# A gated mix of attention and a GLU: SBUF addresses at multiples of 512 bytes, and the splitting of row maxima moved from VectorE to GpSimd with the transpose one period later

## The chip, the cores and the metric

The kernel runs on one core of one Trainium2 chip. The metric is the device time of one execution in microseconds (us). The kernel before took 1719.04 us, the median of 3 runs (1718.17 to 1721.21).

The engines are named as in the profile: PE is TensorE's matmul, PEld its weight load, DVE is VectorE, ACT ScalarE, POOL GpSimd, and SP the queue engine that issues the DMAs.

## What is computed

```python
x = A_x                                              # 2048 tokens, D = 512
g = _sigmoid((x * gate_w).sum(-1, keepdims=True))
a = _A_ref(x, A_wqkv, A_wo)       # softmax attention, 32 heads of 16
b = _B_ref(x, B_w_gate, B_w_up, B_w_down)   # (sigmoid(x Wg) * (x Wu)) Wd, F = 1792
return g * a + (1 - g) * b
```

In the attention, `scores = q k^T * 16 ** -0.5` are taken through a softmax over all 2048 keys, and the result multiplies `v`. All of it is in fp32.

## The kernel before, in words

[...]

The softmax needs the largest score of each row before the exponential. Attention thus makes the scores twice. The first pass (`sm_step`, L271) multiplies queries by keys (PE L284) for 128 queries and 512 keys at a time and takes the maximum of each row (DVE L286). Sixteen such maxima per row block fill one *part*: pair of heads p, chunk c of 512 queries, half b of the pair. There are 16 pairs, 4 chunks and 2 halves, 128 parts. When a part is full, `turn_max` (L294) makes it usable:

- DVE L298 reduces the four key ranges to one maximum for each row, tile `mx`, 128x4;
- DVE L300 casts it to its high half, in the tile `msq`; DVE L301 subtracts to get the low half (both inputs in SBUF);
- DVE L305 transposes 128x128 of `msq` into a tile `mt`, in blocks of 32;
- `send` issues four small DMAs on SP (L311) that put the two halves, as two rows, under the queries in the tile `QS`.

The second pass (`st_part`, L561) multiplies keys by queries (PE L570); with the two extra rows, the matmul itself subtracts the row's maximum. ACT L572 takes the exponential into tiles `p`. `values` (L692) multiplies `p` by v (32 matmuls at PE L702), ACT L707 copies the result out of PSUM, and POOL L720 adds it to a running sum that a DMA later stores.

All of this runs in a main loop of 256 *periods* (k in `range(NPER)`, L774). A period handles 512 queries of two heads against 512 keys: `emit` follows an order written out by hand, in one string for even and one for odd k:

```python
    STEADY = ("m1 t0 t0 d1 d1 m0 t0 d1 d1 m0 m0 d1 d1 t0 work d1 t0 t0 d1 t0 d1 d1 m0 d1 t0 d1 m0 m0 m1",
              "m0 t1 t1 d0 m1 d0 t1 d0 d0 m1 t1 d0 d0 m1 work d0 t1 d0 m1 t1 d0 t1 d0 t1 d0 d0 m1 m1 m0")
```

Here `m0` and `m1` are one step of the first pass for half 0 or 1, `t0` and `t1` one step of the second, `d0` and `d1` two dense matmuls (PE L150 or L170, on half the array each) of the projections and of the GLU, and `work` takes one job from a list, `later`, of small jobs for GpSimd and SP (splits of weights, mixing of operands, sums of products, stores). Each period has eight of the maxima (DVE L286) and eight exponentials. The matmuls of the passes share seven PSUM banks, handed out by a table, `REUSE`.

What ends a period, in this order: `turn_max` for the part that is full (one is, at the end of each odd period), three or four jobs of `later`, then `values(k)`. The `send` of a part is put at the head of `later`, and comes out of it near the end of the next period.

SP takes its DMAs in program order and waits where one has to: for the data that it stores, or for a buffer that it fills.

Ahead of the loop lie dummy matmuls (PE L84), the first projections (PE L137) and the first maxima; there, `turn_max` and its `send` follow at once. The last eight periods have no maxima and no dense work. Behind the loop come the output projections and the GLU's down-projection (PE L137 and L901).

The tiles are placed in SBUF one behind the other in the order of their making. `warm` is 4 bytes wide per partition, and four others that come early (`logit`, `g1`, `g0`, `mx`) are small too, so that the large tiles behind them start at addresses that are 32 over a multiple of 64 bytes. Ahead of all lies a scratch for dynamic transfers, of the default size of 16384 bytes.

Of the kernel before, what the change touches and what calls it, by code (L numbers as in the profile page):

```python
# [12 lines left out]
F32 = mybir.dt.float32  # L13
F32R = mybir.dt.float32r
AF = mybir.ActivationFunctionType
ALU = mybir.AluOpType
# [8 lines left out]
S, D, H, DH, F = 2048, 512, 32, 16, 1792  # L25
P = 128
KT = D // P
NS = S // P
# [21 lines left out]
def gated_mix(ctx, tc, x, xc, xmix, wqk, wv, wo, w_gu, w_down, gate_w, out):  # L50
    nc = tc.nc
    pe, act, dve, pool, sp = nc.tensor, nc.scalar, nc.vector, nc.gpsimd, nc.sync

    ctx.enter_context(tc.manual_schedule(engines=ORDERED))
    keep = ctx.enter_context(tc.tile_pool(name="keep", bufs=1))
# [3 lines left out]
    def turns(tiles):  # L59
        turn = iter(range(1 << 30))  # L60
        return lambda: tiles[next(turn) % len(tiles)]
# [15 lines left out]
    pv_d = dram.tile([NC, NPAIR, P, 256], F32, name="pv_d")  # L77
    rec_d = dram.tile([P, 512], F32, name="rec_d")

    warm = keep.tile([P, 1], F32, name="warm")  # L80
    dve.memset(warm, 0.0)
    z = warm.bitcast(F32R)
    for _ in range(WARM):
        pe.matmul(banks[2], z.to_broadcast([P, P]), z.to_broadcast([P, 512]), start=True, stop=True)  # L84
    den = keep.tile([P, 512], F32, name="den")
    logit = keep.tile([P, NS], F32, name="logit")
    g1 = keep.tile([P, NS], F32, name="g1")
    g0 = keep.tile([P, NS], F32, name="g0")

    def big(name, dt=F32):  # L90
        return keep.tile([P, 2048], dt, name=name, tag="big", bufs=4)

    def mid(name, dt=F32):
        return keep.tile([P, 4, 512], dt, name=name, tag="mid", bufs=3)

    def split(h, l, src, hi, lo):
# [86 lines left out]
    later = []  # L183
# [5 lines left out]
    def work(n):  # L189
        while later and n:  # L190
            later.pop(0)()
            n -= 1
# [3 lines left out]
    QS, KS = zip(*[(big(f"qs{b}", F32R), big(f"ks{b}", F32R)) for b in range(2)])  # L196
# [51 lines left out]
                    yield sp.dma_start((QS, KS)[t][p % 2][r:r + DH, cols].bitcast(F32), src[a, rows, cols])  # L248

    act.activation(g1[:, :1], warm, AF.Exp)  # L250
    square = turns([(keep.tile([P, 4], F32, name=f"mx{i}"), keep.tile([P, 40], F32R, name=f"msq{i}")) for i in range(1)])
    for _ in range(1):
        pool.memset(square()[1].bitcast(F32), 0.0)
    ones = v.rearrange("p t (h c) -> p t h c", c=VW)[:, :, :, DH]
    pool.memset(ones, 1.0)
    q0 = raw_cols(wqk, 0, "q0", act)
# [10 lines left out]
    stat = {}  # L267
# [3 lines left out]
    def sm_step(j):  # L271

        p, s = divmod(j, 32)
        qt, kh = divmod(s, 2)
        qs, ks = QS[p % 2], KS[p % 2]

        def one(b, i):
            part = (p, qt // 4, b)
            if part not in stat:
                stat[part] = keep.tile([P, 4, 4], F32, name=f"stat{p}_{qt // 4}_{b}", tag="stat", bufs=6)  # L280
                count[part] = 0
            r, g = 64 * b, 2 * kh + i
            t = bankm()
            pe.matmul(t, qs[r:r + KM, qt * P:(qt + 1) * P], ks[r:r + KM, g * 512:(g + 1) * 512],  # L284
                      start=True, stop=True)
            dve.tensor_reduce(stat[part][:, qt % 4, g:g + 1], t, axis=AX.X, op=ALU.max)  # L286
            count[part] += 1
            if count[part] == 16:
                full.append(part)
        return one  # L290

    full = []

    def turn_max():  # L294
        part = full.pop(0)
        p, i, b = part
        m, hl = square()
        dve.tensor_reduce(m, stat.pop(part), axis=AX.X, op=ALU.max)  # L298
        two = hl[:, :8].rearrange("p (t c) -> p t c", c=2)
        dve.tensor_copy(two[:, :, 0], m)  # L300
        dve.tensor_tensor(two[:, :, 1], m, two[:, :, 0].bitcast(F32), ALU.subtract)  # L301
        f = hl.bitcast(F32)
        blocks = bass.AP(f.tensor, f.offset, [f.ap[0], (2, 4), (1, 32)])
        mt = keep.tile([P, 4, 32], F32, name=f"mt{p}_{i}_{b}", tag="mt", bufs=2)
        dve.transpose(mt, blocks)  # L305

        def send():
            r = 64 * b + 3 * DH
            rows = QS[p % 2][r:r + 2, i * 512:(i + 1) * 512].bitcast(F32).rearrange("a (t g j) -> a g t j", g=4, j=32)
            for g in range(4):  # L310
                sp.dma_start(rows[:, g], mt[32 * g:32 * g + 2])  # L311
        return send

    SIDES = (slice(0, 64), slice(64, 128))
    def mixing(pair):
# [245 lines left out]
    def st_part(k, b):  # L561

        p, r = divmod(k, 16)
        c, kt = divmod(4 * r, 16)
        qs, ks = QS[p % 2], KS[p % 2]
        r = 64 * b
        pt = ptile[k, b] = mid(f"p{k}_{b}")
        for a in range(4):
            o = bank()
            pe.matmul(o, ks[r:r + KR, (kt + a) * P:(kt + a + 1) * P], qs[r:r + KR, c * 512:(c + 1) * 512],  # L570
                      start=True, stop=True)
            act.activation(pt[:, a, :], o, AF.Exp, scale=DH ** -0.5)  # L572
            yield

    ahead = st_part(0, 1)
    bank = bankm
    for t in range(2, NS, 2):
        two = [Sum(bankv(), tokens(t + a)) for a in range(2)]
        for g in (LOW, UP):
            first_max()  # L580
            for m in range(3 * KT):
                two[0].half(g)
                two[1].half(1 - g)
                if m == 5 or m == 8 and (g == LOW or t == 2):
                    first_max()
                if t == NS - 2 and (g, m) in ((LOW, 8), (UP, 2), (UP, 5), (UP, 8)):
                    next(ahead)
                while full:
                    turn_max()()
            if g == LOW:  # L590
                turn(*two)
            if t >= 12:
                work(1)
        if t < NS - 2:
            for a in range(2):
                put_v(t + a, two[a].o, act)


    seven = [maxb[0], maxb[1], banks[2], maxb[2], banks[1], maxb[3], banks[0]]
    bank7 = turns(seven)  # L600
    chunks = [(c, f) for c in range(NC) for f in range(0, NF, 2)]
# [131 lines left out]
    def dense(g):  # L733
        while True:
            if run:
                run.half(g)
            yield

    count_given = [0]

    def place():
        b = given[-REUSE[count_given[0] % len(REUSE)]]
        count_given[0] += 1
        given.append(b)
        return b

    def emit(order, **parts):

        for word in order.split():
            if word == "turn":  # L750
                if run:
                    turn(run)
            elif word == "work":
                work(1)
            else:
                if next(parts[word], place) is place:
                    place()
# [12 lines left out]
    for a, engine in enumerate((act, dve)):  # L770
        put_v(NS - 2 + a, two[a].o, engine)
    bank = bankm = place
    backlog = []
    for k in range(NPER):  # L774
        n = 2 * k
        if n + FIRST == NSTEP:
            bank = bank7
        if 320 <= n < 448 and n % 16 == 0:
            logit_load((n - 320) // 8)
        if n % 32 == 0 and n // 32 + 1 < NPAIR:  # L780
            pair = load_pair(n // 32 + 1)
        if n % 32 <= 10:
            list(islice(pair, 2))
        if k >= NPER - TAIL:
            group["t0"], group["t1"] = st_part(k, 0), st_part(k + 1, 1) if k + 1 < NPER else iter(())
        elif k % 2 == 0:
            group["t0"] = chain(st_part(k, 0), st_part(k + 1, 0))
        else:
            group["t1"] = chain(st_part(k, 1), st_part(k + 1, 1))
        emit(STEADY[k % 2] if k < NPER - TAIL else LAST[k - NPER], **group)  # L790
        turned = []
        while full:
            turned.append(turn_max())
        if run is None:
            pass
        elif run.done():
            run = next(fill, None)
        else:
            turn(run)
        backlog.append(len(later))  # L800
        work(3 if isinstance(run, Sum) and k % 2 else 4)
        later[:0] = turned
        if 320 <= n < 448:
            t = (n - 320) // 16 * 2
            if n % 16 == 2:
                logit_terms(t, 0)
                logit_terms(t, 1)
            elif n % 16 in (8, 10):
                logit_sum(t, (n % 16 - 8) // 2)
        if EARLY <= k < EARLY + 4:  # L810
            early_exp(*divmod(k - EARLY, 2))
        if k == NPER - 1:
# [78 lines left out]
    for n, (c, f) in enumerate(chunks):  # L891
# [4 lines left out]
        hl = ready[n]  # L896
# [68 lines left out]
```

## Time and profile before

| | |
|---|---|
| median of 3 runs | 1719.04 us (1718.17 to 1721.21) |
| the profiled execution | 1718.9 us |
| its span in the profile | 1717.1 us |
| its mean granted clock | 0.997 |
| PE L702, one period's | 32 matmuls, in 1.92 us |
| DVE L286, the maxima | 2048 of 0.68 us |
| ACT L572, the exponentials | 2048 of 0.63 us |

A row of the timeline reads: start in us from the span's start, length in us, engine, line, operation, out<-in, sizes, how many in a row are merged (x), and in brackets how long the engine stood idle before it and what ended that. A row of a group of instructions reads: line, engine, operation, count | busy us in all, mean ns of one | idle us of the engine just before them. Busy time overlaps itself on PE, because the next matmul begins before the one before it has left the array. The granted clock is the share of its full speed that PE had.

### The profile page before, as it was taken

How to read it: one execution, taken by the hardware profiler on the slowest of the kernel's cores; microseconds unless marked ns; L12 is line 12 of the kernel's file. 1: busy time of each engine (PE TensorE's matmuls, PEld its weight loads, DVE VectorE, ACT ScalarE, POOL GpSimd, SP SyncE). 2: the span in 40 equal slices, each digit the busy share in tenths (PEclk: the TensorE clock that was granted, in tenths of full speed). 3: DMA queues.
4: the chain of work that ended last, by engine and by line, in shares of the span. 5: the costliest groups of instructions: out<-in, count | busy, mean ns of one | idle time of the engine just before them, and what ended most of it. 6: DMA issues, size and time to landing. Idle time of an engine off the chain costs nothing.

```text
span 1717.1 us, 43465 instructions
## 1 busy us (share of the span) xinstructions
PE 1702.4 (99%) x16552; PEld 1129.9 (66%) x16552; DVE 1498.5 (87%) x2706; ACT 1338.0 (78%) x2668; POOL 974.4 (57%) x936
## 2 busy tenths in 40 slices
PE   9999999999999999999999999999999999999999
PEld 7866666666666666666666666666666666578887
DVE  6999999999999999999999999999999999566543
ACT  4188787888888888888888889999888888863321
POOL 1045654347787777766665677677676665252110
PEclk9999999999999999999999999999999999999999
DMA  9524575363544454442347232524242423176752
GB/s 256 113 78 167 164 249 155 114 168 119 137 124 132 134 137 122 128 117 69 100 152 213 85 100 92 120 76 123 64 122 75 104 81 110 42 264 223 238 188 70
DMA packets 125008, 228.54 MB, mean 133 GB/s; under 512 B 19008, under 2 KB 35648, under 8 KB 121792
## 3 DMA queue, kind: packets, MB, share of 16 engines
q1 hardware_dynamic: 124512, 225.24, 45.0%
q8 instruction: 131, 2.15, 0.5%
q14 instruction: 77, 0.63, 0.1%
q10 hardware_dynamic: 288, 0.52, 0.1%
HBM read 149.42 MB, written 75.76 MB: 131 GB/s over the span
## 4 chain that ended last, share of the span: by engine, by line
PE 92%; DVE 6%; DMA 1%; ACT 0%; POOL 0%; issue 0%; SPq 0%; POOLq 0%; ACTq 0%
PE dn L170 26%; PE sm L702 20%; PE sm L284 8%; PE st L284 7%; PE sm L901 7%; PE st L702 6%; PE dn L150 4%; DVE stat L286 4%; PE st L137 4%; PE sm L570 3%; PE st L570 2%; PE dn L901 2%; PE st L150 2%; DVE msq L301 1%; DVE mt L305 0%; PE st L84 0%
## 5 line engine op out<-in xcount | busy, mean ns | idle before, releaser
L286 DVE TENSOR_REDUCE stat<-sm 128x1 f32<-128x512 f32 x1124 | 723.2, 677 | 44.2 <-PE st L570 18.7
L572 ACT ACTIVATE p<-sm 128x512 f32<-128x512 f32 x1217 | 688.4, 631 | 11.3 <-PE sm L570 5.9
L286 DVE TENSOR_REDUCE stat<-st 128x1 f32<-128x512 f32 x924 | 602.2, 676 | 33.6 <-PE sm L570 16.6
L572 ACT ACTIVATE p<-st 128x512 f32<-128x512 f32 x831 | 501.5, 636 | 7.4 <-PE dn L150 3.1
L170 PE MATMUL dn<-xm,mh 64*128 64x512 f32 x1568 | 490.9, 392 | 0.0
L570 PE MATMUL sm<-qs,ks 64*128 64x512 f32 x1217 | 456.2, 411 | 3.8 <-DVE stat L286 3.5
L284 PE MATMUL sm<-ks,qs 48*128 48x512 f32 x1124 | 422.7, 424 | 0.3 <-ACT p L572 0.3
L284 PE MATMUL st<-ks,qs 48*128 48x512 f32 x924 | 369.6, 430 | 0.0
L702 PE MATMUL sm<-p,v 128*17 128x256 f32 x6080 | 366.8, 382 | 0.1
L570 PE MATMUL st<-qs,ks 64*128 64x512 f32 x831 | 331.8, 415 | 5.4 <-DVE stat L286 5.4
L720 POOL TENSOR_TENSOR sum<-sum,part 128x256 f32<-128x256 f32 x192 | 141.3, 736 | 320.0 <-ACT part L707 282.6
L170 PEld LDWEIGHTS dn<-xm,mh 64*128 64x128 f32 x1568 | 290.2, 185 | 42.1
L170 PE MATMUL dn<-xm,ml 64*128 64x512 f32 x784 | 308.8, 394 | 0.0
L702 PEld LDWEIGHTS sm<-p,v 128*17 128x17 f32 x6080 | 160.3, 97 | 166.5 <-ACT p L572 53.7
L284 PEld LDWEIGHTS sm<-ks,qs 48*128 48x128 f32 x1124 | 198.9, 185 | 87.8 <-DVE stat L286 52.7
L570 PEld LDWEIGHTS sm<-qs,ks 64*128 64x128 f32 x1217 | 218.2, 186 | 33.3 <-DVE stat L286 14.6
L284 PEld LDWEIGHTS st<-ks,qs 48*128 48x128 f32 x924 | 165.5, 185 | 84.5 <-DVE stat L286 54.3
L403 POOL TENSOR_TENSOR m<-m,m 128x512 f32<-128x512 f32 x140 | 178.1, 1287 | 4.8 <-ACT m L505 4.8
L570 PEld LDWEIGHTS st<-qs,ks 64*128 64x128 f32 x831 | 152.4, 185 | 26.8 <-DVE stat L286 14.0
L170 PEld LDWEIGHTS dn<-xm,ml 64*128 64x128 f32 x784 | 144.6, 184 | 17.7
L123 POOL TENSOR_TENSOR ml<-r,mh 128x512 fp32r<-128x512 f32 x112 | 143.9, 1285 | 7.7
L505 ACT ACTIVATE m<-dn 128x512 f32<-128x512 f32 x196 | 134.0, 684 | 0.0
(225 smaller groups left out, 2201.0 us busy)
## 6 DMA issues: line engine op xcount, KB each, us to landing
r<-in_w_gu_dram SPq DMA_DIRECT2D x112, 256.0 KB
gul<-gu_d SPq DMA_DIRECT2D x56, 512.0 KB
gu_d<-m SPq DMA_DIRECT2D x84, 256.0 KB
xm_d<-xm SPq DMA_DIRECT2D x32, 512.0 KB
xm<-xm_d SPq DMA_DIRECT2D x32, 512.0 KB
xm<-in_xmix_dram SPq DMA_DIRECT2D x24, 512.0 KB
qs<-q_d SPq DMA_DIRECT2D x90, 128.0 KB
ks<-k_d SPq DMA_DIRECT2D x90, 128.0 KB
```

What stands on the lines that cost most here:

```text
L123: pool.tensor_tensor(l, src, h.bitcast(F32), ALU.subtract)
L150: mm = pe.matmul(self.o, a[rows], b[rows], start=(self.n == 0), stop=(self.n == 2 * len(self.ops) - 1))
L170: pe.matmul(self.o, a, b, start=(self.n == 0), stop=(self.n == len(self.ops) - 1))
L284: pe.matmul(t, qs[r:r + KM, qt * P:(qt + 1) * P], ks[r:r + KM, g * 512:(g + 1) * 512], start=True, stop=True)
L286: dve.tensor_reduce(stat[part][:, qt % 4, g:g + 1], t, axis=AX.X, op=ALU.max)
L403: pool.tensor_tensor(o, x, y, op)
L505: leave = lambda e, o: act.activation(e, o, AF.Copy)
L570: pe.matmul(o, ks[r:r + KR, (kt + a) * P:(kt + a + 1) * P], qs[r:r + KR, c * 512:(c + 1) * 512], start=True, stop=True)
L572: act.activation(pt[:, a, :], o, AF.Exp, scale=DH ** -0.5)
L702: pe.matmul(o[r:r + VW, :], v[:, 4 * k % 16 + a, h * VW:(h + 1) * VW], pts[b][:, a, 256 * i:256 * i + 256], start=(a == 0), stop=(a == 3))
L720: pool.tensor_tensor(s, s, e, ALU.add)
L901: pe.matmul(down[t], a, b, start=(f == 0 and m == 0), stop=(f == NF - 2 and m == 5))
```

## The change

It has three parts.

1. *Addresses and scratch.* `warm` is padded to 96 columns; `logit`, `g1` and `g0` become rows of one tile `gates`; the maxima and their halves lie in one tile `mxs` with two slots of 64 columns (the maximum in columns 40 to 43, the halves in 0 to 7), where `mx` and `msq` were one each. The scratch for dynamic transfers is 2048 bytes. All tiles now start at multiples of 512 bytes. There are 8 buffers for `stat` in place of 6.
2. *Who splits.* `turn_max` falls into `close_max` (the row maximum, on VectorE as before), `halves` (the cast and the subtraction, now on GpSimd, by `split`) and `turned` (the transpose on VectorE), which hands back `send`.
3. *When.* The row maximum stays at the end of odd period k. `halves` goes into a new list, `urgent`, which the next `work` word (in period k + 1) empties ahead of `later`. The transpose stands at the end of period k + 2, ahead of the row maximum of the part that is full there. Its `send` goes into `urgent` too, and comes at the `work` word of period k + 3. Ahead of the loop, one part at a time is closed, halved at once, and transposed and sent four steps later.

With `send` out of `later`, one place more in it is free in every second period, and the jobs behind it come a little earlier in the program.

```diff
-    warm = keep.tile([P, 1], F32, name="warm")
+    warm = keep.tile([P, 96], F32, name="warm")
     dve.memset(warm, 0.0)
+    warm = warm[:, :1]
...
-    logit = keep.tile([P, NS], F32, name="logit")
-    g1 = keep.tile([P, NS], F32, name="g1")
-    g0 = keep.tile([P, NS], F32, name="g0")
+    gates = keep.tile([P, 8, NS], F32, name="gates")
+    logit, g1, g0 = [gates[:, i, :] for i in range(3)]
...
-    square = turns([(keep.tile([P, 4], F32, name=f"mx{i}"), keep.tile([P, 40], F32R, name=f"msq{i}")) for i in range(1)])
-    for _ in range(1):
-        pool.memset(square()[1].bitcast(F32), 0.0)
+    mxs = keep.tile([P, 2, 64], F32R, name="mxs")
+    square = turns([(mxs[:, i, 40:44].bitcast(F32), mxs[:, i, :40]) for i in range(2)])
+    pool.memset(mxs.bitcast(F32), 0.0)
...
-    def turn_max():
+    def close_max():
         part = full.pop(0)
         p, i, b = part
         m, hl = square()
         dve.tensor_reduce(m, stat.pop(part), axis=AX.X, op=ALU.max)
         two = hl[:, :8].rearrange("p (t c) -> p t c", c=2)
-        dve.tensor_copy(two[:, :, 0], m)
-        dve.tensor_tensor(two[:, :, 1], m, two[:, :, 0].bitcast(F32), ALU.subtract)
...
+        def halves():
+            split(two[:, :, 0], two[:, :, 1], m, pool, pool)
+
+        def turned():
+            f = hl.bitcast(F32)
+            blocks = bass.AP(f.tensor, f.offset, [f.ap[0], (2, 4), (1, 32)])
+            mt = keep.tile([P, 4, 32], F32, name=f"mt{p}_{i}_{b}", tag="mt", bufs=2)
+            dve.transpose(mt, blocks)
...
+        return halves, turned
...
             elif word == "work":
+                while urgent:
+                    urgent.pop(0)()
                 work(1)
...
-        turned = []
+        jobs = [turned() for turned in stages.pop(0)]
+        stages.append([])
         while full:
-            turned.append(turn_max())
+            halves, turned = close_max()
+            jobs.append(halves)
+            stages[1].append(turned)
...
-        later[:0] = turned
+        urgent.extend(jobs)
...
-    nc = bacc.Bacc("TRN2", target_bir_lowering=False, num_devices=1)
+    nc = bacc.Bacc("TRN2", target_bir_lowering=False, num_devices=1, dynamic_dma_scratch_size=2048)
```

The lines of the kernel after, for the same things: the row maximum is L298, the halves are L100 and L101 (in `split`), the transpose is L308, the sends L314; the lines behind have moved by 4 (dense loads and sums), by 13 (`values`, L715; the add, L733).

How this stands in the program: first VectorE, at the end of an odd period in which a part of pair 6 is full. The numbers in the names tell the buffers apart; `stat6_0_1` are the sixteen maxima of pair 6, chunk 0, half 1. Before:

```order
L286 TENSOR_REDUCE stat6_0_0_7947<-st0_65 128x1
L298 TENSOR_REDUCE mx0_111<-stat6_0_1_7776 128x4
L300 CAST msq0_112<-mx0_111 128x4
L301 TENSOR_TENSOR msq0_112<-mx0_111,msq0_112 128x4
L305 STREAM_TRANSPOSE mt6_0_1_8064<-msq0_112 128x128
L286 TENSOR_REDUCE stat6_1_1_8095<-st2_67 128x1
```

VectorE after, at the end of a like period of the same pair:

```order
L286 TENSOR_REDUCE stat6_1_0_8255<-st1_66 128x1
L308 STREAM_TRANSPOSE mt6_0_0_8373<-mxs_109 128x128
L298 TENSOR_REDUCE mxs_109<-stat6_1_1_8084 128x4
L286 TENSOR_REDUCE stat6_2_1_8405<-sm1_70 128x1
L286 TENSOR_REDUCE stat6_1_0_8255<-sm0_69 128x1
```

Of the four instructions in a row two are left on VectorE, and the transpose is that of the part before (chunk 0, half 0), ahead of the row maximum of the new one (chunk 1, half 1).

GpSimd after, at a `work` word of an even period, with the two halves between a step of the mixing (L346, L334) and the values' sum (L733):

```order
L346 CAST xm_1_2_6860<-xm_1_2_6860 128x512
L334 TENSOR_TENSOR xm_1_2_6860<-xm_1_2_6860 128x512
L100 CAST mxs<-mxs 128x4
L101 TENSOR_TENSOR mxs<-mxs 128x4
L733 TENSOR_TENSOR sum_3_7044<-sum_3_7044,part_7120 128x256
L407 TENSOR_TENSOR den<-m_0_2_0_7014,m_0_2_0_7096 128x512
```

In GpSimd's order before, neither L100 nor L101 stands at these places.

SP, in pair 1, where the sends of chunk 3, half 0 (`mt_3_0`) stand. Around them are the loads and stores of operands of the dense products (`xm`, `q_d` and `k_d` in HBM). Before:

```order
L722 DMA pv_d<-sum_1_2605 128x256
L311 DMA qs_104<-mt_3_0_2814 2x4x32 x4
L351 DMA xm_1_3614<-xm_d 128x2x512 x2
L331 DMA xm_d<-xm_2_2_2819 256x1x512
L351 DMA xm_1_3614<-xm_d 128x2x512 x2
L321 DMA xm_3_0_3060<-in_xmix_dram 128x512
L238 DMA q_d<-qh_2_2976 128x512
L238 DMA q_d<-qk_1_0_0_2974 128x512
L311 DMA qs_102<-mt_0_1_2972 2x4x32 x4
```

SP after, the same stretch:

```order
L735 DMA pv_d<-sum_1_2597 128x256
L355 DMA xm_0_3126<-xm_d 128x2x512
L355 DMA xm_1_3603<-xm_d 128x2x512 x2
L335 DMA xm_d<-xm_2_2_2737 256x1x512
L355 DMA xm_1_3603<-xm_d 128x2x512 x2
L325 DMA xm_3_0_3051<-in_xmix_dram 128x512
L238 DMA q_d<-qh_2_2965 128x512
L238 DMA q_d<-qk_1_0_0_2963 128x512
L314 DMA qs_102<-mt_3_0_2960 2x4x32 x4
```

The sends of chunk 3, half 0 now stand where those of the next pair's chunk 0, half 1 stood: behind the loads and stores of one more turn.

More of the change, by code (lines that the diff above doesn't have):

```diff
@@ L279, in one @@
             if part not in stat:
-                stat[part] = keep.tile([P, 4, 4], F32, name=f"stat{p}_{qt // 4}_{b}", tag="stat", bufs=6)
+                stat[part] = keep.tile([P, 4, 4], F32, name=f"stat{p}_{qt // 4}_{b}", tag="stat", bufs=8)
                 count[part] = 0
@@ L299, in turn_max, with send @@
         two = hl[:, :8].rearrange("p (t c) -> p t c", c=2)
[L300 to L312, printed above, removed]
+        def halves():
[5 more added lines that the diff above has]
+            dve.transpose(mt, blocks)
+            def send():
+                r = 64 * b + 3 * DH
+                rows = QS[p % 2][r:r + 2, i * 512:(i + 1) * 512].bitcast(F32).rearrange("a (t g j) -> a g t j", g=4, j=32)
+                for g in range(4):
+                    sp.dma_start(rows[:, g], mt[32 * g:32 * g + 2])
+            return send
+        return halves, turned
     SIDES = (slice(0, 64), slice(64, 128))
@@ L573, in st_part @@
             yield
+    closed = []
     ahead = st_part(0, 1)
@@ L587, in gated_mix @@
                     next(ahead)
-                while full:
-                    turn_max()()
+                if closed:
+                    closed[0][0] -= 1
+                    if closed[0][0] == 0:
+                        closed.pop()[1]()()
+                elif full:
+                    halves, turned = close_max()
+                    halves()
+                    closed.append([4, turned])
             if g == LOW:
@@ L596, in gated_mix @@
                 put_v(t + a, two[a].o, act)
+    for _, turned in closed:
+        turned()()
     seven = [maxb[0], maxb[1], banks[2], maxb[2], banks[1], maxb[3], banks[0]]
@@ L737, in dense @@
             yield
+    urgent = []
     count_given = [0]
@@ L772, in gated_mix @@
     bank = bankm = place
-    backlog = []
+    stages = [[], []]
     for k in range(NPER):
@@ L790, in gated_mix @@
         emit(STEADY[k % 2] if k < NPER - TAIL else LAST[k - NPER], **group)
-        turned = []
+        jobs = [turned() for turned in stages.pop(0)]
+        stages.append([])
         while full:
-            turned.append(turn_max())
+            halves, turned = close_max()
+            jobs.append(halves)
+            stages[1].append(turned)
         if run is None:
@@ L799, in gated_mix @@
             turn(run)
-        backlog.append(len(later))
         work(3 if isinstance(run, Sum) and k % 2 else 4)
-        later[:0] = turned
+        urgent.extend(jobs)
         if 320 <= n < 448:
```

## The prediction

> **What bounds the kernel now.** I read the page first: its totals, then the chain that ended last.
>
> ```profile
> PE 1702.4 (99%) x16552; PEld 1129.9 (66%) x16552; DVE 1498.5 (87%) x2706; ACT 1338.0 (78%) x2668; POOL 974.4 (57%) x936
> PE 92%; DVE 6%; DMA 1%; ACT 0%; POOL 0%; issue 0%; SPq 0%; POOLq 0%; ACTq 0%
> ```
>
> PE looks full, but its spans overlap and hide waiting. So I took the loop's beat: from the first L702 matmul of a period to the next one's. The timeline around 902 us, ACT's rows and the L702 rows:
>
> ```profile
> 902.44 1.92 PE L702 MATMUL sm<-p,v 128*17 128x256 f32 x32
> ...
> 904.43 0.39 ACT L707 ACTIVATE sum<-sm 128x256 f32<-128x256 f32 x1 [0.81 <-PE sm L702]
> ...
> 904.83 0.69 DVE L286 TENSOR_REDUCE stat<-sm 128x1 f32<-128x512 f32 x1 [0.48 <-PE sm L570]
> ...
> 904.87 1.08 ACT L572 ACTIVATE p<-sm 128x512 f32<-128x512 f32 x2
> ...
> 907.27 1.62 ACT L572 ACTIVATE p<-st 128x512 f32<-128x512 f32 x3
> ...
> 907.96 1.00 PEld L702 LDWEIGHTS st<-p,v 128*17 128x17 f32 x24 [0.31 <-ACT p L572]
> ```
>
> The period takes 907.96 - 902.44 = 5.52 us. It closes through PE and ACT: 1.99 until ACT copies the values, 0.44 to the next exponential, 2.40 from the first of six to the last (907.27), 0.69 until PE may go on. VectorE waits 0.48 within it for PE. So in an undisturbed period faster work on VectorE gains nothing: 5.52 is the floor.
>
> How far is the loop above it? L702 in a window that ends before the period at 1454.11, and the periods after it:
>
> ```profile
> L702 PE MATMUL sm<-p,v x5824: 379/379/393, 90.3 to 1450.1; 128*17 128x256 f32 x195
> L702 PE MATMUL st<-p,v x1952: 379/379/393, 95.8 to 1444.6; 128*17 128x256 f32 x196
> 1454.11 1.43 PEld L702 LDWEIGHTS sm<-p,v 128*17 128x17 f32 x32 [0.31 <-ACT p L572]
> 1462.41 0.15 PEld L702 LDWEIGHTS sm<-p,v 128*17 128x17 f32 x8 [0.65 <-ACT p L572]
> 1469.62 1.43 PEld L702 LDWEIGHTS sm<-p,v 128*17 128x17 f32 x32 [0.31 <-ACT p L572]
> ```
>
> (5824 + 1952) / 32 = 243 periods in 1454.11 - 90.3 = 1363.8 us; at 5.52 they would take 1341.4. Excess: 22.4 us. The next two take 8.30 and 7.21, which is 4.5 over. All that can be had in the loop is 26.9 us.
>
> Where it arises shows in one period, 315.31 to 321.98 (6.67 us):
>
> ```profile
> 315.31 1.92 PE L702 MATMUL sm<-p,v 128*17 128x256 f32 x32
> ...
> 317.08 0.17 DVE L298 TENSOR_REDUCE mx<-stat 128x4 f32<-128x16 f32 x1
> ...
> 317.47 1.29 POOL L236 TENSOR_TENSOR qk<-qk,qh 128x512 fp32r<-128x512 f32 x1
> 317.49 1.29 DVE L301 TENSOR_TENSOR msq<-mx,msq 128x4 fp32r<-128x4 f32 x1
> ...
> 319.76 0.50 PE L570 MATMUL st<-qs,ks 64*128 64x512 f32 x1 [0.48 <-DVE stat L286]
> ...
> 321.98 0.41 PE L702 MATMUL sm<-p,v 128*17 128x256 f32 x4
> ```
>
> VectorE's subtraction of 4 columns runs 1.29 us and ends with a GpSimd instruction that began 0.02 before it. The maxima behind it come late, a PSUM bank comes free late, PE stands. All 128 of these small instructions, first from the view of single lines (minimum, median, maximum in ns), then from the groups by line (busy us, mean ns):
>
> ```profile
> L301 DVE TENSOR_TENSOR msq<-mx,msq x128: 162/164/1308, 61.8 to 1481.8; 128x4 fp32r<-128x4 f32 x128
> L300 DVE CAST msq<-mx x128: 169/170/819, 61.6 to 1481.6; 128x4 fp32r<-128x4 f32 x128
> L305 DVE STREAM_TRANSPOSE mt<-msq x128: 311/311/315, 62.0 to 1482.0; 128x128 f32<-128x128 f32 x128
> L301 DVE TENSOR_TENSOR msq<-mx,msq 128x4 fp32r<-128x4 f32 x128 | 37.0, 289 | 4.4
> L300 DVE CAST msq<-mx 128x4 fp32r<-128x4 f32 x128 | 28.2, 220 | 4.5
> ```
>
> The halves are stretched, by (289 - 164) x 128 = 16.0 and (220 - 170) x 128 = 6.4, together 22.4 us; the transpose never is.
>
> The two long periods come from the largest case, and something follows it: the timeline, then two windows (length; busy time of PE, PEld, DVE, ACT, POOL; granted clock, DMA share, GB/s):
>
> ```profile
> 1456.09 0.82 DVE L300 CAST msq<-mx 128x4 fp32r<-128x4 f32 x1
> ...
> 1456.94 1.21 DVE L301 TENSOR_TENSOR msq<-mx,msq 128x4 fp32r<-128x4 f32 x1
> ...
> 1459.13 0.79 PE L570 MATMUL st<-qs,ks 64*128 64x512 f32 x1 [1.25 <-DVE stat L286]
> 1454.00:1459.00 5.00, 3.88 (x42) 2.06 (x40) 4.86 (x10) 3.97 (x9) 3.40 (x4) 1.00 0.52 180
> 1459.00:1466.00 7.00, 6.87 (x42) 3.44 (x42) 4.44 (x8) 2.69 (x5) 3.41 (x4) 0.51 0.27 90
> ```
>
> Stretched by 1.70 us in sum; PE stands 1.25 and runs the next 7 us at a granted clock of 0.51.
>
> **The change, part by part.** *Halves to GpSimd.* This removes both stretched instructions from VectorE. In the first 243 periods the stretching is 22.4 - 1.7 = 20.7 of the 22.4 excess; of the unexplained 1.7 I give half, 0.8. At 1456 the whole 4.5 goes if the stall brought the clock down; if the clock fell for a reason of its own, 4.5 - 1.7 = 2.8 stays. The fall begins with the stall, so I count it in. Gain: 20.7 + 0.8 + 4.5 = 26.0. The 0.33 us of unstretched halves gain nothing more: ACT's loop hides them.
>
> [...]
>
> What are GpSimd's copies worth? No row has 128x4 there. The nearest groups of the page and of the groups by line, and GpSimd's fullest window (POOL's 168.93 is the fifth busy time):
>
> ```profile
> L720 POOL TENSOR_TENSOR sum<-sum,part 128x256 f32<-128x256 f32 x192 | 141.3, 736 | 320.0 <-ACT part L707 282.6
> L403 POOL TENSOR_TENSOR m<-m,m 128x512 f32<-128x512 f32 x140 | 178.1, 1287 | 4.8 <-ACT m L505 4.8
> L127 POOL CAST mh<-r 128x512 fp32r<-128x512 f32 x112 | 68.2, 609 | 4.6
> 430.00:645.00 215.00, 214.72 (x2322) 137.34 (x2316) 202.25 (x389) 188.69 (x387) 168.93 (x164) 1.00 0.47 132
> ```
>
> On the line through the first two, 4 columns take 736 - 252 x 551 / 256 = 0.19 us; a cast perhaps 0.15. That is 0.35 a turn, 0.74 + 0.61 = 1.35 at most. One turn per 11.04 us adds 3% (at most 12%) to an engine busy 168.93 of 215 us in its fullest stretch. The cast also waits there for the row maximum, which VectorE reaches 1.77 us after the L702 of its period (317.08 against 315.31). Behind both stand GpSimd's sums, splits and mixings, which go out through SP to readers periods away. GpSimd does not close the loop, so I cost all this at nothing; without that cover it would be 1.35 x 123 turns, some 166 us. [...]
>
> *Transpose one period further on.* On VectorE it stands ahead of the next chunk's row maximum (order of instructions, front part). It waits for GpSimd's halves and for the sends from two turns before. Behind a late one stand that row maximum and eight L286 reductions, and PE waits for their banks. From the row maximum (317.08 in the case above) to the next turn is 11.04 us, less 0.35 for the halves: GpSimd may be over 10 us behind. I cost it at nothing.
>
> *Sends later.* The four DMAs now leave two periods later on SP's queue, behind everything issued in between. For half b=0 that leaves 1.5 periods, 8.3 us, before scores read those rows. One place looks tight: pair 1, chunk 3, b=0. In the new order its send stands behind a load and two stores that ran in before like this (timeline of SP and PE, then a window):
>
> ```profile
> 237.92 1.97 SPq L351 DMA_DIRECT2D xm<-xm_d  x2
> 244.84 0.34 SPq L321 DMA_DIRECT2D xm<-in_xmix_dram  x1
> ...
> 246.22 2.76 SPq L311 DMA_DIRECT2D qs<-mt  x4
> 247.23 0.50 PE L570 MATMUL st<-qs,ks 64*128 64x512 f32 x1
> 219.00:248.00 29.00, 29.00 (x318) 18.69 (x311) 27.19 (x52) 23.95 (x50) 17.44 (x20) 1.00 0.93 292
> ```
>
> SP is held from 239.89 to 244.84 with the DMA engines 93% busy. Four sends at that place end at 248.98; the reader is at 247.23. That is 1.75 us late or more, with the landing perhaps 3. I take it as even odds: 1.3 us. Bounds: nothing, and 3 plus a clock fall like that at 1462 (2.8), 6 in all.
>
> *Opening.* Four turns at 61 to 80 us lose their 0.33 on VectorE: below 0.5, counted as nothing.
>
> *Addresses, scratch.* No operation of before runs at both alignments, so the trace has no price. The nearest: dummy matmuls on the small `warm` tile against the down-projection's.
>
> ```profile
> 5.17 1.48 PE L84 MATMUL st<-warm 128*128 128x512 f32 x6
> 1520.00:1620.00 100.00, 100.00 (x434) 81.29 (x433) 63.11 (x51) 38.26 (x38) 28.07 (x11) 1.00 0.76 252
> ```
>
> Five steps in 1.48 less the last one's 0.38 (a matmul's length in the L702 rows) give 0.22 us; 100 us / 434 gives the real ones 0.230. That is at best 0.01 on each of 295 / 0.230 = 1280 matmuls in the 295 us ahead of and behind the loop, where PE sets the pace: 13 us. No row ties this to addresses, and a dummy reads one column repeatedly, so I take zero and keep the 13 for the low side. DMAs could only gain where they are waited for: 1% of the chain. A loss has the same bound, and the rows speak no more for it.
>
> **Sum.** The profiled execution took 1718.9 us (span 1717.1), 0.1 under the median of 1719.04. 1718.9 - 26.0 + 1.3 = 1694.2, so 1694.
>
> **The rivals.** *Late sends everywhere (slower).* If SP is held at each b=0 part as it was at 240, every such part (64) makes PE wait. It decides once SP runs 8.3 - 2.76 = 5.5 us behind. Break-even is 24.7 / 64 = 0.4 us each; at 1 us each, 1694 + 64 = 1758. For it: 4.95 us of holding seen above. Against: that stretch is the fullest of DMA; in the row at 430 the share is 0.47. 5%.
>
> *The wait changes its name.* GpSimd, fuller now, brings the halves late and some transposes wait for it, or the clock falls all the same. It needs a GpSimd over 10 us behind; its longest work rows quoted average 1.29 us, so eight of them in a row. With a third of the gain lost, 1703; the clock alone, 1697. 10%.
>
> *The change does nothing.* The stretching may only stand beside a wait for a bank that would be there anyway; then 1716 to 1719. Against it: 6.67 - 5.52 = 1.15 equals 1.29 - 0.164. 4%.
>
> *Matmuls gain from the addresses.* In the stages ahead of and behind the loop, 1694 - 13 = 1681. For it only the two rows above; against it, nothing that rows show. 10%.
>
> **How the numbers follow.** The forecast has 71%. Its own range: 1718.9 - 26.9 = 1692 with no late send, to 1718.9 - 20.7 + 3 = 1701. To hold 8 in 10 I reach down most of the way into the addresses' case, 1684, and up to the clock staying plus a late send, 1703. About 0.2% (3.4 us) is what a measurement here can tell from nothing. Faster: 71 + 10 + 10 = 91%; same: 4%; slower: 5%.
>
> **What would show it.** Right: periods of 5.52 nearly throughout, none of 6.67; row maximum and transpose on VectorE at 0.16 and 0.31; about 0.35 us of GpSimd per turn; no clock of 0.51 near 1440. Wrong: PE waiting on DMA at L570 in many periods (late sends); VectorE waiting on GpSimd at the transpose; a step below 0.225 us between the down-projection's matmuls (addresses).

## The result, and the profile after

The kernel after took 1692.05 us (median of 4 runs, 1691.60 to 1693.82), beside 1720.12 for the kernel before (median of 4, the three runs of above and one more, 1718.17 to 1724.67). The ratio, here and below that of the means of the runs, is 0.9835, with a 95% interval of 0.9814 to 0.9856. The forecast was 1694, in a range of 1684 to 1703. The profiled execution took 1691.6 us, its span 1689.8. In 4 of the 39 runs of the kernel before that stood beside the experiments the mean granted clock was 1.000 and the time 1715.7 to 1716.1 us: the fall of the clock that the profile of before shows at 1459 (some 7 us at half speed, which alone bring the mean to 0.998) was absent there.

The page's totals and its chain, in answer to those of before:

```profile
PE 1681.1 (99%) x16552; PEld 1153.2 (68%) x16552; DVE 1431.6 (85%) x2450; ACT 1335.4 (79%) x2668; POOL 1017.9 (60%) x1192
PE 98%; DMA 1%; ACT 1%; DVE 1%; SPq 0%; issue 0%; POOL 0%; ACTq 0%
```

VectorE is 67 us less busy and GpSimd 43 more. VectorE's share of the chain that ended last fell from 6% to 1%.

The loop's beat, as before: all L715 matmuls (the values) from the first period to that at 1446.6, by the view of single lines:

```profile
L715 PE MATMUL sm<-p,v x5888: 379/379/393, 89.6 to 1442.6; 128*17 128x256 f32 x197
L715 PE MATMUL st<-p,v x1952: 379/379/392, 95.1 to 1426.1; 128*17 128x256 f32 x196
1446.60 1.92 PE L715 MATMUL sm<-p,v 128*17 128x256 f32 x32
1452.08 1.92 PE L715 MATMUL sm<-p,v 128*17 128x256 f32 x32
```

(5888 + 1952) / 32 = 245 periods in 1446.6 - 89.6 = 1357.0 us. The same 245 took 1469.6 - 90.3 = 1379.3 before. So the loop gave 22.3 us. What lies ahead of it gave 0.7 (89.6 against 90.3), and what lies behind that point 4.3 (1689.8 - 1446.6 = 243.2, against 1717.1 - 1469.6 = 247.5). Together 27.3: the whole difference of the spans.

At 5.52 us, 245 periods are 1352.4. So 4.6 us of excess are left, against 26.9 before; and one period has all of it and a little more, from 238.70 to 249.06 (10.36 us). (The median period is 5.519 before and 5.517 after; with 5.518 in place of 5.52, the excess is 5.1 and 27.4. From here on the excess is counted over 5.518.) The timeline of SP and PE there, and two windows (length; busy time of PE, PEld, DVE, ACT, POOL; granted clock; DMA share; GB/s):

```profile
238.34 0.34 SPq L325 DMA_DIRECT2D xm<-in_xmix_dram  x1
238.70 1.92 PE L715 MATMUL sm<-p,v 128*17 128x256 f32 x32
...
239.73 2.77 SPq L314 DMA_DIRECT2D qs<-mt  x4
...
244.09 0.46 PE L574 MATMUL st<-qs,ks 64*128 64x512 f32 x1 [3.04 <-DMA qs<-mt]
...
249.06 1.27 PE L715 MATMUL sm<-p,v 128*17 128x256 f32 x20
241.00:244.00 3.00, 0.05 (x1) 0.00 (x0) 0.69 (x1) 0.13 (x1) 2.69 (x5) 1.00 0.46 151
244.00:249.00 5.00, 4.91 (x27) 4.39 (x27) 2.51 (x4) 3.73 (x8) 0.12 (x1) 0.66 0.68 237
```

This is the send of pair 1, chunk 3, half 0: SP was held by the load until 238.34, the four sends were issued by 242.50, and PE stood 3.04 us for them. Over the next five microseconds the mean granted clock was 0.66. Of the 4.85 us that the period has too much, 3.04 are that wait; the other 1.8 lie in the window with the lower clock.

Everywhere else the stretching is gone. The same sort of turn as the one at 315 us before, with the same long GpSimd instruction beside it:

```profile
311.59 0.30 DVE L308 STREAM_TRANSPOSE mt<-mxs 128x128 f32<-128x128 f32 x1
...
311.81 0.13 DVE L298 TENSOR_REDUCE mxs<-stat 128x4 f32<-128x16 f32 x1
312.10 1.29 POOL L236 TENSOR_TENSOR qk<-qk,qh 128x512 fp32r<-128x512 f32 x1
312.31 0.69 DVE L286 TENSOR_REDUCE stat<-st 128x1 f32<-128x512 f32 x1 [0.37 <-PE st L574]
...
313.34 0.18 POOL L100 CAST mxs<-mxs 128x4 fp32r<-128x4 f32 x1
313.61 0.20 POOL L101 TENSOR_TENSOR mxs<-mxs 128x4 fp32r<-128x4 f32 x1
```

VectorE now waits for PE (0.37), not PE for VectorE. All 128 turns:

```profile
L100 POOL CAST mxs<-mxs x128: 178/188/209, 61.2 to 1458.7; 128x4 fp32r<-128x4 f32 x128
L101 POOL TENSOR_TENSOR mxs<-mxs x128: 202/203/207, 61.5 to 1459.0; 128x4 fp32r<-128x4 f32 x128
L298 DVE TENSOR_REDUCE mxs<-stat x128: 124/127/160, 61.0 to 1458.5; 128x4 f32<-128x16 f32 x128
L308 DVE STREAM_TRANSPOSE mt<-mxs x128: 297/301/313, 61.8 to 1464.6; 128x128 f32<-128x128 f32 x128
  POOL mxs L101: 1.7, 3
```

No instruction of the turn is stretched any more: the longest of these 512 takes 0.31 us, where 1.31 stood before. The last row is the transposes' idle time: they waited for GpSimd's halves three times, 1.7 us in all.

Behind the loop, a window for the one quoted of before (434 matmuls in 100 us):

```profile
1500.00:1600.00 100.00, 100.00 (x443) 82.81 (x442) 67.59 (x53) 39.48 (x40) 25.68 (x11) 1.00 0.76 256
```

PE makes 443 matmuls in 100 us, one per 0.2257 us in place of 0.2304. The work there, its order and its DMA share are as before. That is the gain of 4.3 us behind the loop, and it asks for a cause.

### The profile page after: what moved, and what is told of

It is laid out like the page before. It is cut to its first block, busy times and chain, and to the rows that moved or that the text cites. A ratio compares the mean times of both kernels' runs of the same rounds, so it can differ in the third digit from the quotient of the medians.

```text
span 1689.8 us, 43420 instructions
## 1 busy us (share of the span) xinstructions
PE 1681.1 (99%) x16552; PEld 1153.2 (68%) x16552; DVE 1431.6 (85%) x2450; ACT 1335.4 (79%) x2668; POOL 1017.9 (60%) x1192
## 4 chain that ended last, share of the span: by engine, by line
PE 98%; DMA 1%; ACT 1%; DVE 1%; SPq 0%; issue 0%; POOL 0%; ACTq 0%
PE dn L170 23%; PE sm L715 21%; PE sm L284 9%; PE st L284 9%; PE st L715 7%; PE sm L919 7%; PE dn L150 6%; PE sm L574 4%; PE st L137 4%; PE st L574 3%; PE dn L919 2%; PE st L150 1%; ACT p L576 0%; DMA xm<-xm_d 0%; DVE stat L286 0%; PE st L85 0%
## 5 line engine op out<-in xcount | busy, mean ns | idle before, releaser
L170 PE MATMUL dn<-xm,mh 64*128 64x512 f32 x1568 | 485.6, 389 | 0.0
L574 PE MATMUL sm<-qs,ks 64*128 64x512 f32 x1217 | 445.5, 404 | 0.3 <-ACT p L576 0.2
L715 PE MATMUL sm<-p,v 128*17 128x256 f32 x6080 | 365.1, 380 | 0.1
L574 PE MATMUL st<-qs,ks 64*128 64x512 f32 x831 | 325.7, 409 | 3.0 <-DMA qs<-mt 3.0
L170 PE MATMUL dn<-xm,ml 64*128 64x512 f32 x784 | 304.0, 388 | 0.0
L715 PEld LDWEIGHTS sm<-p,v 128*17 128x17 f32 x6080 | 160.3, 97 | 169.4 <-ACT p L576 58.4
L733 POOL TENSOR_TENSOR sum<-sum,part 128x256 f32<-128x256 f32 x192 | 141.7, 738 | 86.9 <-ACT part L720 63.4
L100 POOL CAST mxs<-mxs 128x4 fp32r<-128x4 f32 x128 | 24.1, 188 | 219.6 <-DVE mxs L298 219.3
```

The source lines that it names most:

```text
L170: pe.matmul(self.o, a, b, start=(self.n == 0), stop=(self.n == len(self.ops) - 1))
L715: pe.matmul(o[r:r + VW, :], v[:, 4 * k % 16 + a, h * VW:(h + 1) * VW], pts[b][:, a, 256 * i:256 * i + 256], start=(a == 0), stop=(a == 3))
L733: pool.tensor_tensor(s, s, e, ALU.add)
```

## The experiments

Two theories stood at the start: the loop's gain comes from taking the two small instructions off VectorE, where GpSimd blocks them, and the gain behind the loop comes from the addresses. Their rivals: the stretching needs the old addresses, or the delay of the transpose is what helps, or the gain behind the loop comes of something else.

**The addresses alone.** The kernel before with the padded tiles, `gates`, one slot of `mxs`, 8 buffers for `stat` and the small scratch:

```diff
-    warm = keep.tile([P, 1], F32, name="warm")
+    warm = keep.tile([P, 96], F32, name="warm")
...
+    mxs = keep.tile([P, 2, 64], F32R, name="mxs")
+    square = turns([(mxs[:, 0, 40:44].bitcast(F32), mxs[:, 0, :40])])
...
```

> The kernel before with the addresses of the change alone (all tiles at multiples of 512 bytes, the smaller scratch); splitting, transpose and sends as before. Theory: the stage behind the loop and the opening are paced by PE, and there the addresses shorten the step between two matmuls from 0.2304 to 0.2257 us, 4.3 + 0.7 us in all, while the loop is paced by ACT and by the stalls on VectorE, which stay: 1720 - 5 = 1715, loop periods of 6.67 us as before, 443 matmuls in 100 us behind the loop. Rival: the 4.3 us come from elsewhere (fewer VectorE rows, an earlier store): then 1720 and 434 matmuls in 100 us. Second rival: the stalls need the old address of the halves (32 over a multiple of 64): then they go here too, about 1693.

Measured: 1713.96 us beside 1719.31, a ratio of 0.9975 (0.9962 to 0.9988). Behind the loop and for the stretched instruction:

```profile
1520.00:1620.00 100.00, 100.00 (x443) 82.81 (x442) 67.57 (x53) 37.44 (x39) 27.03 (x10) 1.00 0.75 252
L301 DVE TENSOR_TENSOR mxs<-mxs 128x4 fp32r<-128x4 f32 x128 | 36.9, 288 | 4.4
```

The 443 matmuls are there, and so is the stretching (mean 288 ns, 289 before). The addresses give the part behind the loop, 4 to 5 us, and take nothing from the stalls.

**The halves back on VectorE, the rest as after.**

```diff
+        split(two[:, :, 0], two[:, :, 1], m, dve, dve)
+
         def halves():
-            split(two[:, :, 0], two[:, :, 1], m, pool, pool)
+            pass
```

> The kernel after with cast and subtraction back on VectorE, right behind the row maximum, as before; addresses, two slots, the later transpose and the later sends stay. Theory (VectorE's halves are blocked while GpSimd reads SBUF): periods of 6.5 to 6.7 us come back at those turns where a long GpSimd instruction runs beside them; L101 again up to 1.3 us and its mean near 0.29; 22 to 27 us lost: 1714 to 1719. Rival (the gain is that the transpose no longer waits right behind, or the order of the sends): stays at 1692 to 1696, with stretched halves hidden.

Measured: 1715.48 us, ratio 0.998 (0.9971 to 0.9989). One turn, then the two groups by line:

```profile
106.31 1.92 PE L717 MATMUL sm<-p,v 128*17 128x256 f32 x32
...
108.48 1.29 POOL L236 TENSOR_TENSOR qk<-qk,qh 128x512 fp32r<-128x512 f32 x1
108.56 1.23 DVE L101 TENSOR_TENSOR mxs<-mxs 128x4 fp32r<-128x4 f32 x1
...
112.68 1.92 PE L717 MATMUL sm<-p,v 128*17 128x256 f32 x32
L101 DVE TENSOR_TENSOR mxs<-mxs 128x4 fp32r<-128x4 f32 x128 | 48.4, 378 | 4.4
L100 DVE CAST mxs<-mxs 128x4 fp32r<-128x4 f32 x128 | 27.4, 214 | 4.4
```

The period is 6.37 us long, and the stretching is (378 - 164) x 128 + (214 - 170) x 128 = 33 us, more than the 22.4 before: about as many turns are stretched as before (44 and 42, counting those over 0.05 us), but by more each, 0.75 us on average in place of 0.53. Not all of it reaches the loop, whose excess is 28.3 us. 23 us of the gain are lost. So later transposes and sends bring nothing by themselves; the place of the halves does it. Taken with the run above, the address plays no part in the stretching. The trace shows which instructions are stretched: L101 ends with GpSimd's instruction (109.79 and 109.77), and the casts take up to 1.14 us where their median is 0.17, while the row maxima take 0.13 us in the mean and the transposes 0.30. In the kernel before, too, no row maximum took more than 0.172 us and no transpose more than 0.315. Why the one kind is stretched and the other is not, no run shows.

**No delay.** GpSimd's halves at once, the transpose at once behind them:

```diff
             halves, turned = close_max()
-            jobs.append(halves)
-            stages[1].append(turned)
+            halves()
+            jobs.append(turned())
```

> The kernel after with the halves on GpSimd issued at once behind the row maximum and the transpose at once behind them, at the end of the same period (outside the loop as in after); sends one period later at the work word. Theory: the stretching stays away, but VectorE now waits in each turn for GpSimd, at least its two rows of 0.19 and 0.20 us and up to 1.3 to 2.6 us more where a long GpSimd instruction is running: the delay is what hides this, and without it the time is 1700 to 1730. Rival (the delay is not needed, VectorE has room): about 1687, as with one period.

Measured: 1702.57 us, ratio 0.9906 (0.9887 to 0.9924). The transposes' idle time in all, and the worst turn:

```profile
  POOL mxs L101: 70.0, 115
934.31 1.29 POOL L380 TENSOR_TENSOR r<-r,r 128x512 f32<-128x512 f32 x1 [6.45 <-DMA r<-in_w_gu_dram]
...
937.41 0.31 DVE L308 STREAM_TRANSPOSE mt<-mxs 128x128 f32<-128x128 f32 x1 [3.32 <-POOL mxs L101]
...
938.35 0.79 PE L574 MATMUL sm<-qs,ks 64*128 64x512 f32 x1 [2.25 <-DVE stat L286]
936.00:943.00 7.00, 4.75 (x30) 3.13 (x33) 5.06 (x9) 3.29 (x7) 6.84 (x10) 0.65 0.56 176
```

VectorE now waits for GpSimd in 115 turns of 128, 70 us in all. Most of these cost a period 0.17 us or less, since VectorE has room; the loop's excess is 19.6 us in the profiled execution (which took 1706.37 us, the longest of the four), of which 5.6 come at this one turn and the fall of the clock behind it. The delay is needed: against the version that follows, with one period of it, 15 us.

**One period of delay in place of two.**

```diff
-    stages = [[], []]
+    stages = [[]]
...
-            stages[1].append(turned)
+            stages[0].append(turned)
```

> The kernel after with the transpose at the end of the next period in place of the one after it, and the sends at the work word of period k + 2 in place of k + 3. Theory: the one late send (pair 1, chunk 3, half 0; a period of 10.37 us) goes, since it now stands ahead of the load that holds SP: 4.9 us less; GpSimd's halves have some 4 us for being late, which is mostly enough: about 1687 to 1689. Rival: GpSimd is often more than 4 us behind, VectorE waits for it at the transpose, and PE behind it: 1692 or more, with rows of idle time at L308 released by L101.

Measured: 1687.29 us, ratio 0.9814 (0.9801 to 0.9828). SP in the stretch where the send was late, and the transposes' idle time:

```profile
229.73 2.98 SPq L314 DMA_DIRECT2D qs<-mt  x4
237.12 0.33 SPq L325 DMA_DIRECT2D xm<-in_xmix_dram  x1
...
241.20 2.74 SPq L314 DMA_DIRECT2D qs<-mt  x4
  POOL mxs L101: 2.3, 4
```

The send now goes out at 229.73, ahead of the load that holds SP until 237.12, and the long period is gone: the excess of the whole loop is 0.5 us. GpSimd is late for four transposes, 2.3 us in all, hidden. This beats both kernels. It was run once more beside the kernel after on the same chip:

> The kernel after once more, beside the version with the transpose one period on, on the same chip: 1692, with one period of 8 to 12 us where the sends of pair 1, chunk 3, half 0 come late.

> The version with the transpose one period on, once more beside the kernel after. Theory: 4 to 6 us below it, since its loop has no late send and stands at the floor of 5.52 us: 1687. Rival: the first difference came of two chips or two days: within 1 us of it.

Measured: 1692.82 (1691.97 to 1695.16) and 1688.03 (1686.68 to 1688.77); ratios to before 0.9844 (0.983 to 0.9859) and 0.9811 (0.9798 to 0.9825). The runs of the two don't overlap; the difference is 4.8 us. In this run of the kernel after, the late send made a period of 11.43 us, where 10.36 stood in the first.

**What it is about the addresses.** The first step moves all tiles of the kernel after up by 32 bytes:

```diff
+    keep.tile([P, 8], F32, name="pad")
     warm = keep.tile([P, 96], F32, name="warm")
```

> The kernel after with a pad of 32 bytes per partition ahead of all tiles, so that every tile starts 32 bytes over a multiple of 512; the rest as after. Theory (addresses set the matmuls' step where PE sets the pace): about 434 to 435 matmuls in 100 us behind the loop, 1692 + 5 = 1697; the loop as in after. Rival (addresses do nothing): 443 in 100 us and 1692. Second rival (the stalls depend on the address): the periods of 6.67 come back in part, up to 1715.

```profile
1500.00:1600.00 100.00, 100.00 (x443) 82.81 (x442) 68.66 (x53) 37.42 (x38) 26.20 (x10) 1.00 0.76 255
```

Measured: 1693.76 us and 443 matmuls. The first theory fell here: a start at a multiple of 512 is not what counts, since nothing starts there any more. By the sizes and the order of the tiles, the streaming operands and the loaded ones lay at different places within 512 bytes in the kernel before: `wd_h` and `xt` at 416, `weights` at 352, `hl`, `wd0h` and `q0h` at 32, `oh` at 416. The new theory is that the two operands of a matmul must lie alike. Two kernels test it: tiles behind `stat` moved by 384 bytes alone, and all tiles moved by 416. A third has the smaller scratch alone in the kernel before, and with it all tiles 14336 bytes lower, the one rival that is left.

```diff
-                stat[part] = keep.tile([P, 4, 4], F32, name=f"stat{p}_{qt // 4}_{b}", tag="stat", bufs=8)
+                stat[part] = keep.tile([P, 4, 4], F32, name=f"stat{p}_{qt // 4}_{b}", tag="stat", bufs=14)
```

> The kernel after with 14 buffers for stat in place of 8, so that the tiles behind them in SBUF (xt, wd_h, oh, ol among them) start 384 bytes over a multiple of 512, and those ahead (weights, hl, the split weights wd0h and q0h) stay at multiples of 512. Theory (what counts is that the two operands of a matmul lie alike, modulo some power of two up to 512): the products whose operands now differ (wd_h by hl, weights by oh, xt by q0h) go from 0.2266 to 0.230 us or more, those that still agree (weights by hl, wd0h by hl) stay at 0.2266: about 1695 to 1697. Rival (what counts is the address of the operand that streams, by itself): wd_h by hl and xt by q0h slow down, weights by oh does not. Second rival (the old addresses were slow for another reason): all stay at 0.2266.

Measured: 1698.52 us, a little over the 1695 to 1697 expected, ratio 0.9884 (0.9865 to 0.9903), 435 matmuls in the window. The timeline of PE, for 18 matmuls of `weights` by `hl` (both at 0), then 24 of `wd_h` and `wd_l` (the two halves of one operand, at 384) by `hl` (0), then 24 of `weights` (0) by `oh` and `ol` (again two halves, at 384). The operand named first streams, the tile `weights` too; the second is loaded:

```profile
1503.95 4.24 PE L919 MATMUL sm<-weights,hl 128*128 128x512 f32 x18
1508.03 0.40 PE L919 MATMUL dn<-wd_h,hl 128*128 128x512 f32 x1
...
1513.62 0.40 PE L919 MATMUL dn<-wd_h,hl 128*128 128x512 f32 x1
...
1574.74 0.63 PE L137 MATMUL st<-weights,oh 128*128 128x512 f32 x2
...
1580.11 0.39 PE L137 MATMUL st<-weights,ol 128*128 128x512 f32 x1
```

(1508.03 - 1503.95) / 18 = 0.2267 us where the operands lie alike; (1513.62 - 1508.03) / 24 = 0.2329 where they don't; and (1580.11 - 1574.74) / 23 = 0.2335 from the first to the last start of the third group, where the operand that streams lies at 0 and the loaded one at 384. So it isn't the streaming operand's own address, but the difference.

> The kernel after with a pad of 416 bytes per partition ahead of all tiles, so that every tile starts 416 bytes over a multiple of 512, as the slow streaming operands wd_h and xt did before. Theory (the two operands of a matmul must lie alike): nothing changes, 0.2266 us and about 1692 to 1694, as with the pad of 32. Rival (a start at 416 is slow by itself): 0.232 us for all products, 434 matmuls or fewer in 100 us behind the loop, about 1698.

The edit is the pad of `shift32`'s diff with 104 columns in place of 8.

```profile
1500.00:1600.00 100.00, 100.00 (x443) 82.84 (x442) 67.12 (x53) 40.52 (x41) 26.38 (x10) 1.00 0.74 252
```

Measured: 1691.82 us, ratio 0.9841 (0.9825 to 0.9856), 443 matmuls. A start at 416, slow before, costs nothing if both operands have it.

> The kernel before with the smaller scratch alone; all tiles move down by 14336 bytes and keep their place within 512. Theory: no part of the gain: 1719 to 1720, 434 matmuls in 100 us behind the loop. Rival (the scratch or the lower addresses made the matmuls faster): 443 and about 1715.

```diff
-    nc = bacc.Bacc("TRN2", target_bir_lowering=False, num_devices=1)
+    nc = bacc.Bacc("TRN2", target_bir_lowering=False, num_devices=1, dynamic_dma_scratch_size=2048)
```

```profile
1520.00:1620.00 100.00, 100.00 (x434) 81.29 (x433) 67.82 (x51) 38.11 (x38) 27.05 (x11) 1.00 0.74 250
```

Measured: 1718.72 us, ratio 0.9995 (0.9983 to 1.0007), 434 matmuls. The scratch is no part of it.

Last, the size that counts, with 12 buffers for `stat`, a difference of 256:

> The kernel after with 12 buffers for stat, so that xt, wd_h, oh and ol start 256 bytes over a multiple of 512 and the rest at multiples of 512. If the two operands must agree modulo 256: all products stay at 0.2266 us. If modulo 512: wd_h by hl and weights by oh take 0.230 us or more, weights by hl and wd0h by hl 0.2266.

```profile
1513.01 0.39 PE L919 MATMUL dn<-wd_h,hl 128*128 128x512 f32 x1
...
1518.45 0.39 PE L919 MATMUL dn<-wd_h,hl 128*128 128x512 f32 x1
```

One run, 1692.96 us: 24 matmuls in 5.44 us, 0.2267 each. A difference of 256 is as good as none, one of 384 (128 beyond 256) is not: of the two rules, that of 256 bytes holds for the differences tried. The kernel before fits this (`weights` by `hl` differ there by 320, `wd_h` by `hl` by 384), in the timeline of PE:

```profile
1525.15 4.28 PE L901 MATMUL sm<-weights,hl 128*128 128x512 f32 x18
...
1529.27 0.40 PE L901 MATMUL dn<-wd_h,hl 128*128 128x512 f32 x1
...
1534.86 0.39 PE L901 MATMUL dn<-wd_h,hl 128*128 128x512 f32 x1
```

4.12 / 18 = 0.2289 us for the first, 5.59 / 24 = 0.2329 for the second, and neither at 0.2267. `weights` by `oh`, 64 apart, takes (1601.32 - 1595.95) / 23 = 0.2335 there.

## Why the prediction was right, point by point

The sum of the prediction came to 1694.2. By the trace it is 1718.9 - 27.1 (the loop's stalls) + 4.85 (the late send) - 4.3 - 0.7 (addresses, behind and ahead of the loop) = 1691.6, which is what it took. The 0.7 ahead of the loop is the least sure of these: the first values come at 89.1 to 90.3 us in the ten kept traces whose operands lie alike, and at 90.3 to 90.8 in the other three.

- *The floor and the excess* were right. The period is 5.52 us before and after, with 4% fewer busy microseconds on VectorE. 245 of them take 1351.9 at 5.518; before stood 27.4 us above that, after 5.1, of which 4.85 are the late send. So 27.1 us of stalls went, where 26.0 were forecast: the stretching carried through nearly one for one, and the half of the unexplained 1.7 us that the prediction gave up came as well.
- *The fall of the clock at 1459* went with its stall, as taken; the clock there is 1.00 now. Here falls stand behind stalls of PE of 1.25, 2.25 and 3.04 us. But the runs bear out only the outcome, not that the stall brought the clock down: not every run of the kernel before had the fall, a longer stall (2.47 us) had none behind it, and one fall came without a stall (last section). What brought it at 1459 is not shown.
- *GpSimd's price* was 0.35 us a turn by estimate and 0.188 + 0.203 = 0.39 measured, costing the loop nothing. The cast's 0.15 in it was the author's guess, and took 0.188. Against VectorE's 0.164, the subtraction of four columns is 1.24 times as long on GpSimd.
- *The transposes' waits* were costed at nothing; three of 128 waited, 1.7 us in all. The runs without the delay show that this is the delay's doing.
- *The late send* was placed rightly and mis-sized: 1.3 us in the sum, 4.85 in the trace. The lateness itself was read well. SP was held for longer than before (6.1 us, 232.26 to 238.34, against 4.95), but the sends were issued by 242.50, 1.45 us after PE could have gone on (244.09 - 3.04 = 241.05), where 1.75 was forecast; with the landing it made 3.04, where the prediction has "perhaps 3". The 1.25 us that this leaves for the landing were the author's guess, for which no row was quoted; here it is 3.04 - 1.45 = 1.59. The step that fell short is the even odds, together with the clock, which stood in the bound alone. The send came late in each of six runs with the two-period delay and the halves on GpSimd, in periods that were 2.9 to 6.6 us too long, and 1.8 of the 4.85 here lie in the window with the lower clock.
- *The addresses* were mis-sized too: zero was taken, with 13 us as the bound and 10% as the chance, and 5.0 came. The bound's row, the dummy matmuls, was no price for it: its 0.22 us was not reached by the products at any address tried. The step that failed is "no operation of before runs at both alignments". Pairs of operands did, in the same stage: `weights` by `hl` and `wd_h` by `hl` lay differently to each other, and their steps stood apart in the trace (0.2289 and 0.2329, above).

The two errors, +3.5 and -5.0, had opposite signs; together with the 1.1 us of the stalls they leave 2.6 us between 1694.2 and 1691.6. The main term, the stalls, was right in where it came from; that the two errors nearly cancelled is luck. The rival of late sends everywhere did not come about: in the rest of the loop no period is more than 0.2 us over the floor.

## What to carry to other kernels

Here casts and subtractions of four columns on VectorE, which paces PSUM banks, could cost not their own 0.16 to 0.17 us but up to the length of the GpSimd instruction beside them, 1.3 us. Moved to GpSimd, they need a consumer late enough to hide its queue (one period of 5.5 us was enough here: four waits in 128 turns, 2.3 us in all, hidden), and no later, since the DMAs behind that consumer have a due time of their own (with two periods one send came late, for 4.85 us). When operands of matmuls are placed in SBUF and PE sets the pace, let both start at the same place modulo 256 bytes, as long as nothing else is measured: a step took 0.2267 us here with the operands 0 or 256 bytes apart, and 0.2289 to 0.2335 with 64, 320 or 384. Small odd tiles in between break that. Before giving a term no price, look for the same operation on two tiles whose addresses differ.

## What the runs showed of the hardware

Matmuls (128 rows of weights, 512 columns streaming, in fp32r) whose two operands start alike modulo 256 bytes were issued every 0.2267 us. With a difference of 384 bytes it was every 0.2329 to 0.2335, 3% longer, whichever of the two was moved; with 320 bytes it was 0.2289, and with 64 bytes 0.2335. It made 4 to 5 us of 1720, where PE sets the pace. That difference could be measured only there, and why it costs is not settled by these runs: they show the steps for the differences tried, not the mechanism.

The granted clock was 0.51 to 0.66 in windows of 5 to 7 us behind PE stalls of 1.25 us (before, at 1459), 2.25 us (without the delay, at 938) and 3.04 us (after, at 244). It was 1.00 behind stalls of 0.48 us (before, at 320) and 0.51 us (before, at 250), and behind one of 2.47 us (all tiles moved by 416, at 244); and it fell to 0.50 for 3.4 us in the second run with one period of delay, at 1454, where PE had not waited more than 0.25 us at a time in the 14 us before:

```profile
243.93 0.47 PE L575 MATMUL st<-qs,ks 64*128 64x512 f32 x1 [2.47 <-DMA qs<-mt]
244.00:249.00 5.00, 5.00 (x55) 3.92 (x59) 4.10 (x7) 4.03 (x8) 2.01 (x3) 1.00 0.61 220
1454.00:1457.40 3.40, 3.40 (x30) 1.68 (x23) 0.57 (x3) 1.37 (x4) 0.84 (x3) 0.50 0.02 5
```

The first two rows are of the kernel moved by 416, the third of the run with one period. What brings the clock down stays open.
